# Attention with part of the exponentials on VectorE: four shifted bit patterns summed on TensorE in place of a polynomial, and x transposed by DMA

## The chip, the cores and the metric

One core of one Trainium2 chip. The metric is the time of one execution in microseconds (us), on the device; lower is better. Beside each time stands the mean clock that was granted to TensorE, as a share of full speed: a core at 0.5 all the time multiplies matrices at half speed.

A run is called "slow" here when it is more than 1.5% above the fastest run of the same kernel in its series. On one core that label is no more than this comparison.

The clock is recorded only from its first rise on, which lies between 3.8 and 20.9 us in these traces. Before that the views print full speed, although groups of products follow each other at 0.42 us there, as at half clock. So the mean clocks below are a little too high: with half clock up to the first record, before is 0.614 (not 0.626).

## The reference

```python
B, S, D, H = 1, 2048, 448, 16          # Dh = 28
qkv = (x @ wqkv).reshape(B, S, 3, H, Dh) -> q, k, v      # all bf16
scores = einsum("bhqd,bhkd->bhqk", q, k) * Dh ** -0.5
o = einsum("bhqk,bhkd->bhqd", softmax(scores), v)
return o.reshape(B, S, D) @ wo
```

There are 16 heads of 2048 x 2048 scores, so 67 million exponentials. In tiles of 128 keys by 512 queries that is 1024 tiles. The work is cut into 16 units, each of four heads and 512 queries: 16 key blocks of four tiles, one for each head.

## The kernel before

A small scheduler in the kernel (`P.add`) gives each operation an engine, what it depends on and a priority, and works out the order of each engine. A score tile is one matmul that uses 28 of the 128 rows of the array; three heads run side by side in different row strips. ScalarE takes the exponential of three such tiles in one instruction:

```python
s = P.add("pe", (lambda e, tl=tl, b0=b0: s_mm(e, tl, range(b0, b0 + 3), DH)), ...)
ex = P.add("act", (lambda e, p0=p0, w=w, b0=b0:
           e.activation(PT[:, p0*512:(p0+w)*512], bank(b0, w), AF.Exp, scale=ESCALE)), ...)
```

ScalarE alone would be the bound, so 114 of the 1024 tiles go to VectorE, where a cubic polynomial in the fraction and the integer part make up the bit pattern of a bf16. It takes five instructions for each tile:

```python
o1: DT = min(max(score, ZLO), ZHI)          # PSUM read, to int32
o2: DW = DT.low16 * ES + EC                 # fraction
o3: DU = (DW + EA) * DW
o4: DU = (DU + EB) * DW
o5: PD = DT * (1/512) + DU                  # int16, read as bf16
```

The products with V follow, for a key block at a time: four matmuls side by side, each over 128 rows and in one strip of 32 columns. The same accumulator bank gathers all 16 key blocks of a unit, and a column of ones in V gives the sum of the exponentials.

```python
ins = e.matmul(ps[32*h:32*h+32, ACC*512:(ACC+1)*512], V[:, kt, hh*32:(hh+1)*32],
               p_ap, start=(kt == 0), stop=(kt == NK-1), tile_position=(0, 32*h))
```

x arrives in its natural order and TensorE transposes it through PSUM, the memory that its products are written to: 64 transposes in 16 groups of four.

Of the kernel before, what the change touches and what calls it, by code (L numbers as in the profile page):

```python
# [58 lines left out]
class _Prog:  # L59
# [7 lines left out]
    FULL_CLOCK_UNTIL = 0.0  # L67
# [25 lines left out]
    def pe_dur(self, prev, op, t):  # L93

        if op.kind is None:
            return op.dur
        one, switch = (220.0, 100.0) if t < self.FULL_CLOCK_UNTIL else (430.0, 110.0)
        if prev is None or prev.kind != op.kind:
            return switch + one * op.units
        if op.kind == "r" and op.heads and not set(op.heads) & set(prev.heads):  # L100
            return 60.0
        return one * op.units
# [155 lines left out]
ES = 3.285997142359445e-05  # L258
EC = 27.848949706562973
EA = -77.30729786983042  # L260
EB = 1961.0831047043987
ZLO = -127.0 * 65536.0
ZHI = 128.0 * 65536.0 - 1.0


def _fast(nc, x, wqkv, wo, out, n_heads=16):
# [6 lines left out]
    IT = 112  # L273
    NIT = D // IT
# [7 lines left out]
    NPT = 36  # L282
    NPD = 8
    NDB = 3
# [3 lines left out]
    QSCALE = 65536.0 * LOG2E * scale  # L288
    ESCALE = 1.0 / (65536.0 * LOG2E)
    assert DH * H == D and G * 4 == H and DH + 1 <= 32 and NIT * IT == D and GD <= IT  # L290

# [4 lines left out]
    LATE0, LATE1 = 1, 1  # L296
    ASLACK = 300.0
# [3 lines left out]
    with es:  # L301
# [3 lines left out]
        x_nat = sb("x_nat", [128, NST, D], BF16)  # L305
# [5 lines left out]
        V = sb("V", [128, NK, HC], BF16)  # L311
        PT = sb("PT", [128, NPT * 512], BF16)
        PD = sb("PD", [128, NPD, 512], I16)
        DT = sb("DT", [128, NDB, 512], I32)
        DW = sb("DW", [128, NDB, 512], FP32)
        DU = sb("DU", [128, NDB, 512], FP32)
# [6 lines left out]
        id_b = sb("id_b", [128, 128], BF16)  # L323
# [5 lines left out]
        FLAG = sb("FLAG", [1, 1], I32)  # L329
        ps = es.enter_context(nc.psum_tensor("ps", [128, 8 * 512], FP32))  # L330
# [4 lines left out]
        def bank_bf(b):  # L335
            return ps[:, b * 512:(b + 1) * 512].bitcast(BF16)

        def i32v(ap):
            return ap.bitcast(I32)


        XG = 4
        xv = xf.rearrange("(n p) d -> p n d", p=128)
        wview = wqkv.rearrange("(it p) c -> p it c", p=IT)
        dma_x = []

        def load_x(i, prio):
            n0, n1 = i * NST // XG, (i + 1) * NST // XG
            dma_x.append(P.add("sp", (lambda e: e.dma_start(x_nat[:, n0:n1, :], xv[:, n0:n1, :])),
                               dur=400, prio=prio, name=f"dma_x{i}", dma_group=_DmaGroup(f"x{i}"), nbytes=(n1 - n0) * 128 * D * 2))  # L350
        for i in range(XG):
            load_x(i, -10 + i)
        dma_w = {}
        for t, en, prio in ((1, "act", -20), (0, "act", -19), (2, "sp", -7.5)):
            dma_w[t] = P.add(en, (lambda e, t=t: e.dma_start(w_raw[0:IT, :, t * D:(t + 1) * D], wview[:, :, t * D:(t + 1) * D])),
                             dur=400, prio=prio, name=f"dma_w{t}", dma_group=_DmaGroup(f"w{t}"), nbytes=D * D * 2)


        io_op = P.add("pool", lambda e: e.iota(iota_i[:, :], [[1, 128]], base=0, channel_multiplier=-1),
                      dur=300, prio=-12, name="iota")  # L360
        id_f_op = P.add("dve", lambda e: e.tensor_scalar(id_f[:, :], iota_i[:, :], 0.0, None, ALU.is_equal),
                        deps=[io_op], dur=250, prio=-10, name="id_f")
        id_b_op = P.add("dve", lambda e: e.tensor_copy(id_b[:, :], id_f[:, :]), deps=[id_f_op], dur=150, prio=-10, name="id_b")
        V4 = V.rearrange("p n (hh r) -> p (n hh) r", r=32)
        ms_v0 = P.add("pool", lambda e: e.memset(V4[:, :, DH:32], 0.0), dur=1500, prio=-9, name="ms_v0")
        ms_v1 = P.add("pool", lambda e: e.memset(V4[:, :, VONE:VONE + 1], 1.0), deps=[ms_v0], dur=800, prio=-9, name="ms_v1")
        ms_wop = P.add("pool", lambda e: e.memset(i32v(wop.rearrange("p g d -> p (g d)")), 0), dur=900, prio=-8, name="ms_wop")
        ms_one = P.add("pool", lambda e: e.memset(ONE[:, :], 1.0), dur=100, prio=-7, name="ms_one")
        sel_op = P.add("dve", (lambda e: e.tensor_copy(SEL[:, :], id_f.rearrange("p (h r) -> p h r", r=32)[:, :, VONE])),
                       deps=[id_f_op], dur=100, prio=-6, name="sel")  # L370
        grp_wo = _DmaGroup("wo")
        dma_wo = []
        for g in range(G):
            for h in range(4):
                r0 = (4 * g + h) * DH
                p0 = 32 * h
                dma_wo.append(P.add("sp", (lambda e, g=g, r0=r0, p0=p0: e.dma_start(wop[p0:p0 + DH, g, :], wo[r0:r0 + DH, :])),
                                    deps=[ms_wop], after=dma_wo[-1:] + dma_x[-1:], dur=300, prio=-5, name=f"dma_wo{g}{h}", dma_group=grp_wo))


        P.pool("E", [4, 5, 6])
        P.pool("J", [5, 6])
        P.pool("M", [6])
        early_ev = []
        mid_ev = []
        cur_pool = ["J"]

        def job(name, prio, mm_ops, evac, early, evac_eng="dve", evac_dur=610, after=(), mul=None):

            hold = []  # L390
            prev = None
            pool = "E" if early else cur_pool[0]
            for k, (f, deps, kind, units_) in enumerate(mm_ops):
                op = P.add("pe", (lambda e, f=f: f(e, hold[0].banks[0])),
                           deps=list(deps) + (list(mid_ev if pool == "M" else early_ev) if (k == 0 and not early) else []), after=[prev] + list(after),
                           kind=kind, units=units_, prio=prio if (k == 0 or early) else -4.0, name=f"{name}_{k}", acq=((pool, 1) if k == 0 else None), acq_slack=0.0 if early else ASLACK)
                if k == 0:
                    hold.append(op)
                prev = op
# [6 lines left out]
            ev = P.add(evac_eng, fe, deps=[prev] + list(evac[2:]), dur=evac_dur, prio=prio if early else -100.0, name=f"{name}_ev", rel=[(hold[0], 0)])  # L406
            if pool != "M":
                (early_ev if early else mid_ev).append(ev)
            return ev

        xt_ev = {}

        def tr_job(n0, it, prio, eng):
            def f(e, b):
                ins = None
                for j in range(4):
                    ins = e.transpose(bank_bf(b)[0:IT, j * 128:(j + 1) * 128],  # L417
                                      x_nat[:, n0 + j, it * IT:(it + 1) * IT], id_b[:, :])
                return ins
            xt_ev[(it, n0 // 4)] = job(f"xT{it}_{n0}", prio, [(f, [id_b_op, dma_x[n0 // 4]], "f", 1.1)],  # L420
                                       ((lambda: xT[0:IT, it, n0 * 128:(n0 + 4) * 128]), (lambda b: bank_bf(b)[0:IT, 0:512])),
                                       True, evac_eng=eng, evac_dur=600 if eng == "act" else 420)
# [3 lines left out]
        def proj_qk(t, g, c, prio, early, eng="dve"):  # L426
            dst = KT if t == 1 else QT
            mms = []
            for it in range(NIT):
                def f(e, b, it=it):  # L430
                    ins = None
                    for h in range(4):
                        col = t * D + g * GD + h * DH
                        ins = e.matmul(ps[32 * h:32 * h + 32, b * 512:(b + 1) * 512], w_raw[0:IT, it, col:col + 32],  # L434
                                       xT[0:IT, it, c * 512:(c + 1) * 512], start=(it == 0), stop=(it == NIT - 1), tile_position=(0, 32 * h))
                    return ins
                mms.append((f, [xt_ev[(it, c)]] + ([dma_w[t]] if it == 0 else []), "c", 1.0))
            kq_ev[(t, g, c)] = job(f"p{t}_{g}_{c}", prio, mms,
                                   ((lambda: dst[:, g, c * 512:(c + 1) * 512]), (lambda b: bank(b))), early, evac_eng=eng, mul=QSCALE if t == 0 else None)

        v_ev = {}

        def proj_v(g, c, prio, early):
            mms = []
            for j in range(4):
                n = 4 * c + j

                def f(e, b, j=j, n=n):
                    ins = None
                    for it in range(NIT):  # L450
                        ins = e.matmul(ps[:, b * 512 + j * GD:b * 512 + (j + 1) * GD], xT[0:IT, it, n * 128:(n + 1) * 128],  # L451
                                       w_raw[0:IT, it, 2 * D + g * GD:2 * D + (g + 1) * GD], start=(it == 0), stop=(it == NIT - 1))
                    return ins
                mms.append((f, [xt_ev[(it, c)] for it in range(NIT)] + [dma_w[2]], "f", 1.1))
            Vd = V[:, 4 * c:4 * c + 4, g * 128:(g + 1) * 128].rearrange("p n (h r) -> p n h r", r=32)[:, :, :, 0:DH]
            v_ev[(g, c)] = job(f"pv_{g}_{c}", prio, mms,
                               ((lambda: Vd), (lambda b: bank(b)[:, 0:4 * GD].rearrange("p (n h d) -> p n h d", n=4, d=DH)), ms_v1), early, evac_dur=600)


        for c in range(NCH):  # L460
            for it in range(NIT):
                tr_job(4 * c, it, -3 + 0.25 * c + 0.001 * it if c == 0 else 0.25 * c - 0.35 + 0.001 * it, "act" if (c == 0 and it % 2) else "dve")
            if c == 0:
                proj_qk(0, 0, 0, -2.9, True, "act")
                proj_qk(1, 0, 0, -2.8, True, "dve")
            else:
                proj_qk(1, 0, c, 0.25 * c - 0.3, True)
            proj_v(0, c, 0.25 * c - 0.1, True)
        proj_qk(0, 0, 1, 0.7, True)

        def late_jobs():
            order = [("q", 0, c) for c in range(2, NCH)]
            for g in range(1, G):
                for c in range(NCH):
# [1012 lines left out]
```

## Time and profile before

| | kernel before |
|---|---|
| time, the three first runs | 459.88, 475.35, 478.32 us |
| profiled run | 478.32 us, span 477.6 us, clock 0.626 |
| TensorE busy | 418.7 us, 2985 matmuls |
| ScalarE busy | 419.8 us, 315 exponentials |
| VectorE busy | 387.9 us, 700 instructions |
| first exponential starts, last one ends | 13.1, 456.3 us |

The times fall into two groups, near 460 and near 478, and the profile was taken of a run of the upper group. Three engines are busy above 80%, which tells nothing about which one to relieve.

### The profile page before, as it was taken

The numbers are of one execution on the slowest core, as the hardware profiler recorded it, in microseconds if no ns is written. First come the engines' busy times: TensorE is split into PE (matmuls) and PEld (weight loads), VectorE is DVE, ScalarE is ACT, GpSimd is POOL, SyncE is SP. The second block draws the span as 40 slices with busy tenths as digits, with TensorE's granted clock in tenths as the row PEclk, the third lists the DMA queues.
The fourth block names the chain that finished last, engine by engine and source line by source line (L and its number), as shares of the span: only waits on it lengthen the run. The fifth ranks groups of instructions, "written<-read, shape, count | busy, mean of one in ns | idle before, by whom it ended". The sixth has DMA issues, their size and how long they took to land.

```text
span 477.6 us, 7257 instructions
## 1 busy us (share of the span) xinstructions
PE 418.7 (88%) x2985; PEld 113.1 (24%) x2985; DVE 387.9 (81%) x700; ACT 419.8 (88%) x321; POOL 3.4 (1%) x9
## 2 busy tenths in 40 slices
PE   4999999988999899887999897899888899989775
PEld 2433112121221212121222211121213211122231
DVE  2322499998969899998989899999988899998331
ACT  2766699999999999999999999999999999999810
POOL 2000000000000000000000000000000000000000
PEclk9655555566565657777555758555667756575985
DMA  8100010000000000000001000000001000101111
GB/s 249 32 1 0 1 32 3 1 24 2 23 1 23 3 3 23 3 23 2 25 1 26 1 3 23 15 10 7 19 1 25 0 14 11 26 10 44 49 40 43
DMA packets 13838, 10.09 MB, mean 21 GB/s; under 512 B 5932, under 2 KB 11820, under 8 KB 13800
## 3 DMA queue, kind: packets, MB, share of 16 engines
q1 hardware_dynamic: 12872, 8.78, 6.6%
q10 hardware_dynamic: 928, 0.80, 0.6%
q8 instruction: 24, 0.39, 0.3%
q14 instruction: 14, 0.11, 0.1%
HBM read 7.50 MB, written 2.08 MB: 20 GB/s over the span
## 4 chain that ended last, share of the span: by engine, by line
ACT 41%; PE 40%; DVE 12%; DMA 4%; issue 2%; SPq 0%; ACTq 0%
ACT PT L711 41%; PE ps L698 16%; PE ps L657 8%; PE ps L434 8%; PE ps L451 4%; PE ps L571 3%; DVE DT L731 3%; DVE DU L737 2%; DVE PD L739 2%; DMA w_raw<-in_wqkv_dram 2%; DMA RB<-scr_r 1%; DVE DU L735 1%; PE ps L417 1%; DVE DW L733 1%; DVE OTS L594 1%
## 5 line engine op out<-in xcount | busy, mean ns | idle before, releaser
L711 ACT ACTIVATE PT<-ps 128x1536 bf16<-128x1536 f32 (+1 forms) x315 | 415.6, 1447 | 28.9 <-PE ps L698 26.1
L698 PE MATMUL ps<-QT,KT 28*128 28x512 bf16 x1024 | 208.3, 549 | 42.3 <-ACT PT L711 35.5
L657 PE MATMUL ps<-PT,V 128*32 128x512 bf16 x910 | 132.8, 554 | 0.0
L731 DVE TENSOR_SCALAR DT<-ps 128x512 int32<-128x512 f32 x114 | 78.2, 686 | 15.2 <-PE ps L698 14.7
L698 PEld LDWEIGHTS ps<-QT,KT 28*128 28x128 bf16 x1024 | 40.2, 97 | 209.8 <-ACT PT L711 129.8
L735 DVE SCALAR_TENSOR_TENSOR DU<-DW 128x512 f32<-128x512 f32 x114 | 77.7, 685 | 0.6
L739 DVE SCALAR_TENSOR_TENSOR PD<-DT,DU 128x512 int16<-128x512 int32 x114 | 77.5, 682 | 0.2
L737 DVE SCALAR_TENSOR_TENSOR DU<-DU,DW 128x512 f32<-128x512 f32 x114 | 77.4, 682 | 0.2
L657 PE MATMUL ps<-PD,V 128*32 128x512 bf16 x114 | 61.6, 543 | 0.0
L434 PE MATMUL ps<-xT,w_raw 112*32 112x512 bf16 x512 | 54.7, 556 | 1.9 <-DVE DT L731 0.8
L733 DVE TENSOR_SCALAR DW<-DT 128x512 f32<-128x512 uint16 x114 | 47.3, 420 | 0.6
L657 PEld LDWEIGHTS ps<-PT,V 128*32 128x32 bf16 x910 | 23.9, 102 | 79.0 <-issue 76.1
L451 PE MATMUL ps<-w_raw,xT 112*128 112x112 bf16 x256 | 25.3, 281 | 0.3 <-DVE DT L731 0.3
L405 DVE CAST KT<-ps 128x512 bf16<-128x512 f32 x16 | 11.0, 689 | 15.4 <-PE ps L434 15.2
L583 DVE CAST OUTS<-ps 128x448 bf16<-128x448 f32 x14 | 8.7, 622 | 17.7 <-PE ps L571 17.7
L571 PE MATMUL ps<-wop,OTN 128*128 128x448 bf16 x64 | 20.1, 451 | 3.2 <-DVE OUTS L583 1.2
L451 PEld LDWEIGHTS ps<-w_raw,xT 112*128 112x128 bf16 x256 | 20.8, 134 | 8.5 <-issue 3.9
L405 DVE CAST V<-ps 128x448 bf16<-128x448 f32 x16 | 9.9, 620 | 14.3 <-PE ps L451 14.3
L434 PEld LDWEIGHTS ps<-xT,w_raw 112*32 112x32 bf16 x512 | 14.6, 120 | 27.0 <-issue 16.4
L581 ACT ACTIVATE OUTS<-ps 128x448 bf16<-128x448 f32 x2 | 1.1, 544 | 17.4 <-PE ps L571 17.4
L403 DVE TENSOR_SCALAR QT<-ps 128x512 bf16<-128x512 f32 x15 | 10.3, 687 | 5.4 <-PE ps L434 5.2
L657 PEld LDWEIGHTS ps<-PD,V 128*32 128x32 bf16 x114 | 11.4, 101 | 8.9 <-issue 8.9
(34 smaller groups left out, 68.4 us busy)
## 6 DMA issues: line engine op xcount, KB each, us to landing
RB<-scr_r SPq DMA_DIRECT2D x60, 64.0 KB, 2.0
x_nat<-in_x_dram SPq DMA_DIRECT2D x4, 448.0 KB, 7.9
out_dram<-OUTS SPq DMA_DIRECT2D x16, 112.0 KB, 1.7
w_raw<-in_wqkv_dram ACTq DMA_DIRECT2D x2, 392.0 KB, 6.7
w_raw<-in_wqkv_dram SPq DMA_DIRECT2D x1, 392.0 KB, 9.5
wop<-in_wo_dram SPq DMA_DIRECT2D x16, 24.5 KB
scr_l<-OTS SPq DMA_DIRECT2D x15, 8.0 KB
LT<-scr_l SPq DMA_DIRECT2D x15, 8.0 KB, 1.6
```

The source lines that it names most:

```text
L405: fe = (lambda e: e.tensor_copy(evac[0](), evac[1](hold[0].banks[0])))
L434: ins = e.matmul(ps[32 * h:32 * h + 32, b * 512:(b + 1) * 512], w_raw[0:IT, it, col:col + 32], xT[0:IT, it, c * 512:(c + 1) * 512], start= ...
L451: ins = e.matmul(ps[:, b * 512 + j * GD:b * 512 + (j + 1) * GD], xT[0:IT, it, n * 128:(n + 1) * 128], w_raw[0:IT, it, 2 * D + g * GD:2 * D ...
L571: return e.matmul(bank(hold[0].banks[0])[:, 0:D], OTN[:, gg, n * 128:(n + 1) * 128], wop[:, gg, :], start=(gg == 0), stop=(gg == G - 1))
L657: ins = e.matmul(ps[32 * h:32 * h + 32, ACC * 512:(ACC + 1) * 512], V[:, kt, hh * 32:(hh + 1) * 32], p_ap, start=(kt == 0), stop=(kt == NK ...
L698: ins = e.matmul(bank(b), KT[32 * h:32 * h + rows, g, kt * 128:(kt + 1) * 128], QT[32 * h:32 * h + rows, g, c * QCH:(c + 1) * QCH], start= ...
L711: ex = P.add("act", (lambda e, p0=p0, w=w, b0=b0: e.activation(PT[:, p0 * 512:(p0 + w) * 512], bank(b0, w), AF.Exp, scale=ESCALE)), deps=[ ...
L731: o1 = P.add("dve", (lambda e, T=T, s=s: e.tensor_scalar(T, bank(s.banks[0]), ZLO, ZHI, ALU.max, ALU.min)), deps=[s, d_last[di]], dur=610, ...
L733: o2 = P.add("dve", (lambda e, F16=F16, W=W: e.tensor_scalar(W, F16, ES, EC, ALU.mult, ALU.add)), deps=[o1, d_last[di]], dur=360, prio=pr, ...
L735: o3 = P.add("dve", (lambda e, W=W, U=U: e.scalar_tensor_tensor(U, W, EA, W, ALU.add, ALU.mult)), deps=[o2], dur=610, prio=pr, name=f"D3_{ ...
L737: o4 = P.add("dve", (lambda e, W=W, U=U: e.scalar_tensor_tensor(U, U, EB, W, ALU.add, ALU.mult)), deps=[o3], dur=610, prio=pr, name=f"D4_{ ...
L739: o5 = P.add("dve", (lambda e, U=U, T=T, pi=pi: e.scalar_tensor_tensor(PD[:, pi, :], T, 1.0 / 512.0, U, ALU.mult, ALU.add)), deps=[o4, slo ...
```

## The change

The intent is to take far more of the exponentials away from ScalarE (252 tiles in place of 114) by making one cheaper for VectorE. Read as a bf16, an int16 that grows linearly with the score is a piecewise-linear approximation of an exponential, with an error that repeats with every power of two. Four such patterns, each shifted by a quarter of a power of two (32, 64 and 96 in int16 steps) and weighted, average the error away. The weights go into four scaled copies of V, and TensorE adds the four up in the accumulator. VectorE is left with one read of PSUM for each tile and three cheap 16-bit additions for each four tiles; TensorE gets four V products where it had one.

```diff
+TERM_D = (0, 32, 64, 96)
+TERM_C = (0.25, 0.2099609375, 0.1767578125, 0.1484375)
+ZBIAS = 127.0 * 128.0 - 7.235034912313908
...
-o1 ... o5 (five instructions for each tile)
+r = P.add("dve", e.tensor_scalar(PD[:, zs, 0, h*512:(h+1)*512], bank(...), ZBIAS, 0.0, ALU.add, ALU.max))
+# once the four tiles of the key block are there, for j in 1, 2, 3:
+sh = P.add("dve", e.tensor_scalar(PD[:, zs, j, :], PD[:, zs, 0, :], float(TERM_D[j]), None, ALU.add))
+# and for j in 0 ... 3, head by head:
+pv_mm(e, u, h, VC[:, kt // 4, j, hh*32:(hh+1)*32], PD[:, zs, j, h*512:(h+1)*512].bitcast(BF16))
...
+# which key blocks VectorE takes
+if u == 0: return (3, 7, 15)
+return (3, 7, 11, 15)
...
-tr_job(...)  # TensorE transposes of x and their evictions
+e.dma_start_transpose(xT[:, 0:NIT-1, r0:r1], xf[r0:r1, 0:(NIT-1)*KT_])   # four pairs
...
+for i in range(9):      # all-zero products that start TensorE's clock
+    e.matmul(ps[32*h:32*h+32, ACC*512:(ACC+1)*512], ZW[:, :], ZM[:, :], ...)
...
-P.pool("E", [4, 5, 6]) ; P.pool("J", [5, 6]) ; P.pool("M", [6])
+P.pool("M", [5, 6])     # banks shared by projections, VectorE score tiles, output products
```

ScalarE's groups are now of three and two tiles by turns. Scaling V for the four copies, and the normalising multiply, go to GpSimd.

## The prediction

> **What bounds the kernel now.** I read the page first (busy shares, the slices, the chain), then the groups by shape, then the chain of waits at both ends, then the engines' work in stretches of time.
>
> ```profile
> PE 418.7 (88%) x2985; PEld 113.1 (24%) x2985; DVE 387.9 (81%) x700; ACT 419.8 (88%) x321; POOL 3.4 (1%) x9
> ...
> ACT  2766699999999999999999999999999999999810
> ...
> PEclk9655555566565657777555758555667756575985
> ...
> ACT 41%; PE 40%; DVE 12%; DMA 4%; issue 2%; SPq 0%; ACTq 0%
> ```
>
> Three engines are above 80% busy and the chain is shared by ScalarE (41%) and TensorE (40%). The slices tell them apart by time. From 60 to 444 us ScalarE is at 9 in every slice: there it is the bound. In the first five slices it stands at 6 to 7, and in the last two it is idle. The clock row swings between 5 and 9.
>
> ```profile
> L711 ACT ACTIVATE PT<-ps 128x1536 bf16<-128x1536 f32 x282 | 383.0, 1500 | 14.7 <-PE ps L698 12.4 <-PE ps L657 1.7
> L698 PE MATMUL ps<-QT,KT 28*128 28x512 bf16 x1024 | 208.3, 549 | 42.3 <-ACT PT L711 35.5 <-DVE KT L405 2.3 <-DVE DT L731 1.8
> L657 PE MATMUL ps<-PT,V 128*32 128x512 bf16 x910 | 132.8, 554 | 0.0
> L731 DVE TENSOR_SCALAR DT<-ps 128x512 int32<-128x512 f32 x114 | 78.2, 686 | 15.2 <-PE ps L698 14.7
> ```
>
> Of 1024 score tiles (128x512), ScalarE exponentiates 910, mostly three to an instruction; VectorE does 114 by five instructions each (78.2 + 47.3 + 77.7 + 77.4 + 77.5 = 358 us, 3.14 us a tile). In the timeline 8 ScalarE instructions of three tiles take 10.98 us, so one costs 1.372 us. Check: 282 x 1.372 + 31 x 1.02 (two tiles) + 1 = 420, the busy time.
>
> ```profile
> 24.00:36.00 12.00, 12.00 (x82) 4.79 (x80) 3.21 (x6) 8.18 (x9) 0.00 (x0) 0.50 0.00 1
> ...
> 206.12:209.53 3.41, 3.41 (x33) 1.78 (x30) 3.41 (x7) 3.41 (x3) 0.00 (x0) 0.50 0.24 79
> 209.53:212.95 3.42, 2.47 (x32) 0.73 (x29) 3.42 (x7) 3.20 (x4) 0.00 (x0) 1.00 0.00 0
> ```
>
> The columns are the stretch, its length, then busy us (and instructions) of TensorE, its weight loads, VectorE, ScalarE and GpSimd, then granted clock and DMA. Between 24 and 36 us TensorE is busy all the time at half clock and ScalarE only 8.18 of 12: TensorE bounds the first 60 us. Later the clock jumps between 0.50 and 1.00 on a grid of 3.413 us.
>
> ```profile
> 448.51 5.49 ACT PT L711 x4
> ...
> 462.20 1.98 PE ps L626 x32
> ...
> 474.18 0.54 ACT OUTS L581
> ```
>
> The last exponential ends at 454.0 and the span at 477.6: a tail of 23.6 us.
>
> **What the Trainium skill says.** (1) "TensorE: Matmul & The Clock Gate", Part 1: the clock is half or full, set by activity in windows of about 3.4 us. The trace agrees on both, but plain busy time is not the activity: 12.00 of 12.00 busy stayed at 0.50. I therefore counted, in each of 135 windows, how much array work was streamed, in units of one full 128x128 array over 512 columns (a 28-row score matmul is 0.22, a 32-column V matmul 0.25, and so on). With a limit of 5.8 units the count says what clock the next window gets in 131 of the 135; the mean is 5.04, so this kernel lies just under the limit. (2) "ScalarE: Activation LUTs", What ACT_TABLE_LOAD costs: 186 ns + 0.833 ns an element, with 93 ns of overlap; for 1536 that is 1.373 us, as measured, and for 1024 it gives 0.946. (3) "VectorE: DVE Perf Modes", the perf-mode tier table: a one-source 16-bit SBUF operation over 2048 elements runs four at a time, 693 ns; the trace has none of that kind. (4) "DMA: Bandwidth & Descriptors", table row on DMA transposes: 261 GB/s effective; no run here shows one yet.
>
> **The change part by part.**
>
> *Exponentials.* Unit 0 gives VectorE 3 of its 16 key blocks, the other 15 units give 4: 63 blocks x 4 heads = 252 tiles (114 before). ScalarE keeps 772, in groups of 3 and 2 by turns: 154 x 1.372 + 155 x 0.946 = 358 us, 62 less than 420. This is the gain.
>
> *VectorE.* A block is four PSUM reads (0.60 us apart back to back in the chain) and three shifted copies of 2048 int16. 252 x 0.60 = 151; 189 x 0.60 (estimate: the skill's 693 ns less the 0.09 by which the 686 ns operations overlap) = 114; K and Q evictions 31 x 0.60 = 19, V with its extra copy 12, accumulators 10, outputs 8, reciprocals 4. Sum 318 us against 388: 89% of ScalarE's time. The normalising multiply and the V scaling go to idle GpSimd.
>
> *TensorE.* V groups (four matmuls side by side) rise from 256 to 193 + 4 x 63 = 445. A group streams in 0.427 us at half clock and 0.213 at full (6 groups of the last V products: 1.44 us at full clock, with the fill). At full clock: scores 309 x 0.213 = 66 (the compiled order puts most VectorE score tiles beside a ScalarE group of other heads, nearly free), V 95, K and Q 128 x 0.213 = 27, V projection 14, output 12, end 3: 217; plus some 600 changes of matmul kind at 0.1 us = 60. That is 277 us, hidden under 358. At half clock it is 434 + 60 = 494, which would be the bound.
>
> *The clock.* Array work: scores 224, V 445, K and Q 128, V projection 56, output 56: about 910 units over some 117 windows = 7.8 a window, above 5.8. Where the projections are over (units 11 on, before output products) it is only (2.88 + 1.45) units per 2.318 us of ScalarE = 6.4. So I expect full clock most of the time (0.9 or more) with dips late.
>
> *The start.* Sixteen transposes on TensorE and their evictions go; four pairs of DMA transposes come. Nine dummy products warm the clock. The compiled order has K of block 1 ahead of the first scores, so two x chunks must have landed. I keep the first exponential at 13 us, as before (13.1), but after it the early slices should run at ScalarE's speed, not TensorE's.
>
> *The tail.* The same serial steps, with two PSUM banks for output products where one was (the products 1.67 and evictions 0.64 now overlap) and less half clock: 15 us instead of 23.6.
>
> *Sum.* 13 + 358 + 15 = 386. ScalarE was 96% busy between 60 and 444 us; the new kernel has TensorE at 77%, VectorE at 89% and the two shared banks between them, so I take 96% again: 358 / 0.96 = 373. Total **402 us**.
>
> **Rivals.** *TensorE stays at half clock*: the second-largest sum, 494, becomes the bound and the time is about 500, slower than now. For it: the present kernel holds 0.50 over long stretches with TensorE fully busy. Against: at half clock the V share makes a busy window carry about 0.73 x 8 = 5.9 units, enough to raise it again, and a raised one carries more. A mixture (clock 0.75) gives 415 to 430. *VectorE becomes the bound*: if the int16 copies run one element at a time (2.2 us, from the skill's 1x figure of 2293 ns), VectorE needs 318 + 189 x 1.6 = 620 us. For it: no int16 fast copy in the trace. Against: the condition in the table is 16-bit width. A milder form, GpSimd and VectorE disturbing each other, costs some us. *The DMA transposes are slow*: every us by which chunk 1 lands after about 9 us goes straight into the time; at a third of the rate quoted, 10 us more. *ScalarE loses nothing and was only waiting*: excluded by its 9s.
>
> **Range and chances.** 96% could be 98 (395) or 92 (420); the clock and the start add up to 10 on the bad side. 80%: 388 to 426. The slow rivals together get 4%.
>
> **What would show it.** Right: about 309 exponentials with 358 us busy in all; ScalarE at 9 from the second or third slice on; the clock row mostly 9; V products at about 1780 matmuls with a mean well under 554 ns; the 2048-wide copies near 690 ns; the tail near 15 us. Wrong: a clock row of 5s with TensorE ahead of ScalarE in the chain, or VectorE at 95% and the exponentials waiting for score tiles that wait for a bank, or a first exponential after 18 us.

## The result, and the profile after

| | before | after |
|---|---|---|
| time, four runs each on one chip | 459.88, 475.35, 478.32, 460.60 us | 401.62, 402.29, 400.07, 402.77 us |
| median | 467.98 us | 401.96 us |
| ratio of the fast runs | | 0.874 (0.869 to 0.879) |
| span of the profiled run, clock | 477.6 us, 0.626 | 398.0 us, 0.927 |

A ratio here is the mean time of one kernel's fast runs over that of the other's fast runs of the same rounds. It is therefore not quite the ratio of the medians: the median of before mixes its two groups, the fast runs are those near 460 alone.

The page of the kernel after: busy time, the slices of ScalarE and of the clock, and the shares of the chain of waits.

```profile
PE 348.9 (88%) x3713; PEld 106.6 (27%) x3713; DVE 334.0 (84%) x557; ACT 357.0 (90%) x314; POOL 48.5 (12%) x97
...
ACT  1599999999999999999999999999899999999811
PEclk9899999999999999999968687898689999999886
...
PE 43%; DVE 28%; ACT 24%; DMA 2%; issue 1%; SPq 0%
```

ScalarE stands at 8 or 9 from the third slice until the end of its work; before, the second to fifth slices read 6 and 7 (the first reads 2; the prediction counts it among them). The clock row is made of 9s where it was made of 5s to 7s, with a softer stretch from the 21st to the 30th slice. The chain now goes mostly through TensorE and VectorE although ScalarE is as good as never idle. It is one chain, followed back from the end; where three engines feed one another it can run through any of them, and it does not name the bound here. The slices do.

The groups by shape (busy us, then mean ns of one, then idle time before them and what ended it):

```profile
L741 ACT ACTIVATE PT<-ps 128x1536 bf16<-128x1536 f32 x154 | 231.7, 1505 | 11.4 <-PE ps L704 10.5
L759 DVE TENSOR_SCALAR PD<-ps 128x512 int16<-128x512 f32 x252 | 169.5, 685 | 31.3 <-PE ps L704 29.9
L741 ACT ACTIVATE PT<-ps 128x1024 bf16<-128x1024 f32 x155 | 167.5, 1081 | 0.7 <-PE ps L704 0.4
...
L766 DVE TENSOR_SCALAR PD<-PD 128x2048 int16<-128x2048 int16 x189 | 131.2, 713 | 0.9
L656 PE MATMUL ps<-PD,VC 128*32 128x512 bf16 x1008 | 98.6, 416 | 11.9 <-DVE PD L766 7.9 <-DVE OTS L593 2.4 <-DVE PD L759 0.5
L656 PE MATMUL ps<-PT,V 128*32 128x512 bf16 x772 | 76.5, 408 | 1.1 <-DVE OTS L593 1.1
```

The counts are those that the prediction worked out (154 + 155 exponentials, 252 reads, 189 copies, 1008 + 772 V products). The same V matmul that took 554 ns on average now takes 408: that is the clock, since its shape is unchanged. ScalarE's idle time before its exponentials is 12.1 us in all, where it was 28.9.

The stretch from 24 to 36 us, in the order of columns that the prediction explains:

```profile
24.00:36.00 12.00, 12.00 (x156) 4.42 (x153) 10.12 (x18) 12.00 (x12) 2.60 (x8) 1.00 0.01 3
```

TensorE is busy for the whole stretch, as before, but it does 156 matmuls where it did 82, at a clock of 1.00; ScalarE is busy for 12.00 of 12 us where it was 8.18. Busy time of TensorE said "12.00" in both kernels.

The end of the chain (start, duration, what):

```profile
378.13 4.70 PE ps L570 x16
382.83 0.58 PE ps L656 x8
...
386.73 0.70 DVE OTN L630
387.43 0.05 issue
387.48 4.90 PE ps L570 x16
392.38 0.02 issue
392.40 0.54 ACT OUTS L580
```

The last exponential ends at 379.2 us and the span at 398.0. The tail of 18.8 us holds two sets of output products of nearly 5 us; the first set stands ahead of the last V products.

The profiled runs can be added up. For the kernel before, the tail has to be corrected: the prediction took 454.0 us, the end of the last ScalarE piece on the chain, as the last exponential, but one more, off the chain, ended at 456.3.

| us | before | after | difference |
|---|---|---|---|
| until the first exponential | 13.1 | 13.9 | +0.8 |
| exponentials, busy | 415.6 | 353.8 | -61.8 |
| idle between them | 27.6 | 11.5 | -16.1 |
| after the last one | 21.3 | 18.8 | -2.5 |
| span | 477.6 | 398.0 | -79.6 |

The before of this table is a run of the upper group. Against its fast runs the gain is some 58 us (460.2 to 401.7), and where those runs save their 18 us cannot be read, as none of them has a trace.

### The profile page after: what moved, and what is told of

Read it like the earlier page. It is cut to its first block, busy times and chain, and to the rows that moved or that the text cites. A ratio compares the mean times of both kernels' runs of the same rounds, so it can differ in the third digit from the quotient of the medians.

```text
span 398.0 us, 8639 instructions
## 1 busy us (share of the span) xinstructions
PE 348.9 (88%) x3713; PEld 106.6 (27%) x3713; DVE 334.0 (84%) x557; ACT 357.0 (90%) x314; POOL 48.5 (12%) x97
## 4 chain that ended last, share of the span: by engine, by line
PE 43%; DVE 28%; ACT 24%; DMA 2%; issue 1%; SPq 0%
ACT PT L741 24%; PE ps L656 16%; PE ps L704 16%; DVE PD L759 12%; DVE PD L766 11%; PE ps L430 6%; PE ps L570 2%; PE ps L450 2%; DVE OTS L593 2%; DMA xT<-in_x_dram 2%; DVE QT L410 1%; DVE KT L412 1%; DVE V L412 1%; SPq L349 0%; PE ps L625 0%
## 5 line engine op out<-in xcount | busy, mean ns | idle before, releaser
L741 ACT ACTIVATE PT<-ps 128x1536 bf16<-128x1536 f32 (+1 forms) x309 | 353.8, 1292 | 12.1 <-PE ps L704 10.9
L759 DVE TENSOR_SCALAR PD<-ps 128x512 int16<-128x512 f32 x252 | 169.5, 685 | 31.3 <-PE ps L704 29.9
L704 PE MATMUL ps<-QT,KT 28*128 28x512 bf16 x1024 | 148.2, 407 | 22.6 <-ACT PT L741 19.3
L766 DVE TENSOR_SCALAR PD<-PD 128x2048 int16<-128x2048 int16 x189 | 131.2, 713 | 0.9
L656 PE MATMUL ps<-PD,VC 128*32 128x512 bf16 x1008 | 98.6, 416 | 11.9 <-DVE PD L766 7.9
L656 PE MATMUL ps<-PT,V 128*32 128x512 bf16 x772 | 76.5, 408 | 1.1 <-DVE OTS L593 1.1
L638 POOL TENSOR_TENSOR OTN<-RB,OTS 128x512 bf16<-128x512 f32 x15 | 20.3, 1355 | 199.9 <-DMA RB<-scr_r 199.8
L430 PE MATMUL ps<-xT,w_raw 128*32 128x512 bf16 x512 | 40.7, 397 | 4.4 <-DMA xT<-in_x_dram 4.0
L656 PEld LDWEIGHTS ps<-PD,VC 128*32 128x32 bf16 x1008 | 24.7, 96 | 54.2 <-DVE PD L766 26.8
L465 POOL TENSOR_SCALAR VC<-VX 128x112 bf16<-128x112 f32 x64 | 21.9, 342 | 124.8 <-DVE VX L459 121.8
```

The lines of the kernel that those rows point to most:

```text
L430: ins = e.matmul(ps[32 * h:32 * h + 32, b * 512:(b + 1) * 512], w_raw[:, it, col:col + 32], xT[:, it, c * 512:(c + 1) * 512], start=(it == ...
L465: sc = P.add("pool", (lambda e, dst=dst, j=j: e.tensor_scalar(dst, src, TERM_C[j], 1.0, ALU.mult, ALU.mult)), deps=[ev2, ms_c1[j]], after= ...
L638: nm = P.add("pool", (lambda e: e.tensor_tensor(OTN[:, g, c * QCH:(c + 1) * QCH], RB[:, ub, :], OTS[:, ub, :], ALU.mult)), deps=[l4], dur= ...
L656: return e.matmul(ps[32 * h:32 * h + 32, ACC * 512:(ACC + 1) * 512], lhsT, rhs, start=first, stop=False, skip_group_check=True, tile_posit ...
L704: return e.matmul(bank(b), KT[32 * h:32 * h + DH, g, kt * 128:(kt + 1) * 128], QT[32 * h:32 * h + DH, g, c * QCH:(c + 1) * QCH], start=Tru ...
L741: ex = P.add("act", (lambda e, p0=p0, w=w, b0=b0: e.activation(PT[:, p0 * 512:(p0 + w) * 512], bank(b0, w), AF.Exp, scale=ESCALE)), deps=[ ...
```

## The experiments

Twelve kernels ran. The first series shared a chip and the runs of before there (seven runs, 458.1 to 463.1 us).

One count is used throughout. For every window of 3.413 us (the grid on which the clock changes) I added up the array work that was streamed, in array units (one full 128 x 128 array over 512 columns), as the prediction did, now also with the transposes in it (with them, the kernel before has 5.18 a window; the prediction, without them, had 5.04). The rule "5.8 units or more, and the next window gets the full clock" then tells the next clock right in 1673 of 1731 windows of fourteen traces. The limit was set on the trace of before alone. A recount gave 1697 of 1745; there, "the clock stays as it is" is right in 1449, and the best of six limits tried on TensorE's busy time in 1138. Few windows at half clock are left in the fast kernels (16 in after, 11 in c_d3zero, 9 in a_spread), so their shares in the fifth column rest on little.

| kernel | array units in the windows counted | a window | a window at half clock | of those, followed by full clock | clock |
|---|---|---|---|---|---|
| before | 699 | 5.18 | 4.83 | 13% | 0.626 |
| a_rows72 | 706 | 5.08 | 4.46 | 4% | 0.607 |
| b_dmaT | 715 | 5.34 | 4.92 | 17% | 0.657 |
| a_d2 | 803 | 6.13 | 4.62 | 10% | 0.690 |
| a_d5 | 948 | 6.67 | 5.04 | 17% | 0.745 |
| a_d3 | 862 | 6.74 | 5.28 | 30% | 0.757 |
| b_dummy | 943 | 7.14 | 5.47 | 28% | 0.822 |
| after | 907 | 8.02 | 6.05 | 69% | 0.927 |
| c_d3zero | 1019 | 8.49 | 6.23 | 64% | 0.953 |
| a_spread | 891 | 8.33 | 6.16 | 56% | 0.959 |

(The windows before the first record of the clock are left out of the count. The traces hold all of the products: 713 units for before, 920 for after and for a_spread.)

### a_rows72: the same instructions, fewer rows of the array

Every V product reads 72 of its 128 rows. The result is wrong; the instructions, their columns and their order stay the same (the traces show TensorE's products in the very same order). If the clock follows instructions or busy time, nothing happens; if it follows the filled array, it must fall.

```diff
-return e.matmul(ps[...], lhsT, rhs, start=first, ...)
+return e.matmul(ps[...], lhsT[0:72], rhs[0:72], start=first, ...)
```

> The changed kernel with every V product contracted over 72 of the 128 rows (wrong result on purpose): the same instructions, shapes of output and streaming time, but the array work of a V group falls to 0.56 units. Theory (the clock of the next 3.413 us follows the array work, and the changed kernel needs the clock): late stretches carry (1.62 + 1.45) units per 2.318 us = 4.5 a window, below 5.8, so half clock there and partly before; mean clock 0.6 to 0.75; TensorE then needs 2.6 to 3.2 us per five ScalarE tiles against 2.318, time 425 to 455 us. Rival (the clock follows busy time, or ScalarE hides TensorE at any clock): 402 us and an unchanged clock of 0.93.

Measured: 453.58, 471.76, 483.33 and 495.24 us at clocks of 0.699, 0.652, 0.633 and 0.607: the lower the clock, the longer the run. Even the fastest is 52 us above the kernel after. From the page and the windows of the profiled run (495.24 us):

```profile
PEclk9999555598555555555975555555555555556866
...
L656 PE MATMUL ps<-PD,VC 72*32 72x512 bf16 x1008 | 133.6, 574 | 2.6 <-DVE OTS L593 1.5
L656 PE MATMUL ps<-PT,V 72*32 72x512 bf16 x772 | 104.9, 559 | 0.8 <-DVE OTS L593 0.8
```

```profile
24.00:48.00 24.00, 23.75 (x293) 8.54 (x293) 21.41 (x38) 23.89 (x22) 3.74 (x12) 0.99 0.02 4
48.00:72.00 24.00, 24.00 (x177) 5.82 (x170) 15.64 (x27) 16.54 (x14) 2.40 (x5) 0.50 0.08 18
```

Up to 48 us, while many products of the projections run beside it (119 from 24 to 48 us), the clock is full and ScalarE is at 23.89 of 24. In the next stretch, with 45 of them, TensorE is busy for all of 24.00 us at 0.50, and ScalarE falls to 16.54. So it is the rows of the array that count, and nearly the whole gain of the change hangs on the clock: with the offload in place but the clock lost, the kernel is about where it was before, or slower. The direction and the clock came as expected; the time went above the range in three of four runs. The range was too narrow for the clock that went with it: a mean of 0.6 means half clock for 80% of the time.

### b_dummy: the clock without the offload

The opposite arm. In the kernel before, each V product but a unit's last is followed by a group of four products of zeros, which change no result, and its scheduler is told of a full clock throughout and of V groups that take twice as long, so that TensorE's order changes too.

```diff
+if kt < NK - 1:
+    for h in range(4):
+        ins = e.matmul(ps[32*h:32*h+32, ACC*512:(ACC+1)*512], ZW[:, :], ZM[:, :], start=False, stop=False, ...)
...
-P.FULL_CLOCK_UNTIL = 45000.0
+P.FULL_CLOCK_UNTIL = 1e9
```

> The kernel before with a group of four all-zero V products added behind each V group but a unit's last (240 groups, result unchanged) and its static order made for the full clock. Array work rises from 5.0 to about 6.8 units a window. Theory (clock by array work; the kernel before is bound by ScalarE from 60 us on): clock 0.9 or more, the first 60 us shorten by some 15 us, the tail by 4; the middle stays: 445 to 455 us. Rival (the higher clock is what made the changed kernel fast): 400 to 415 us. Third (zeros do not count as work, the added products only cost): clock 0.6 and 480 us or more.

Measured: 456.48 (fast, clock 0.871), 467.99, 470.08 and 472.42 us (slow, 0.805 to 0.822), beside fast runs of before at 456.98 to 462.48, mean 460.0. Fast against fast that is a ratio of 0.992, from a single fast run.

```profile
ACT  2999898998899999899898999988997999999950
...
PEclk9999795955899597598879979555877989798995
```

The clock rose from 0.63 to 0.82, and ScalarE stands at 8 and 9 from the second slice on, so the early loss is mended. Little came of it. ScalarE still needs 414 us for its exponentials, which with a start of 12.4 and a tail of 17.0 makes 444 even without one idle microsecond. I had expected 445 to 455; it missed that, and the remaining half-clock stretches, in which the zeros themselves take TensorE's time, are in the row above. So a higher clock alone brought some 4 us, by one fast run at 0.871; a clock that is full throughout was not reached, and the sum above leaves some 15 us at most for it. Neither half of the change gains much alone, the two together gain 58.

### a_d2, a_d3: fewer key blocks for VectorE

Two and three key blocks for each unit in place of four (one less in unit 0).

```diff
-    return (3, 7, 15)
-return (3, 7, 11, 15)
+    return (7, 15)                # a_d3;  a_d2: (7,)
+return (3, 7, 15)                 # a_d3;  a_d2: (7, 15)
```

> The changed kernel with half the key blocks on VectorE (2 a unit, 1 in unit 0: 124 tiles, about as many as the kernel before gave it); ScalarE keeps 900 tiles, 180 pairs x 2.318 us = 417 us. Theory (the gain is ScalarE's smaller share): the changed kernel needs 402 for 358 us of ScalarE work, so 36 us of ends and 2% of gaps; here 417 x 1.022 + 36 = 462 us, clock 0.6 to 0.8 because the array work falls to some 6.2 units a window. Rival (the gain is the clock, the DMA transposes or the shorter VectorE sequence, whatever the share): 400 to 415 us.

> 3 blocks a unit (2 in unit 0): 188 VectorE tiles, ScalarE 836 = 387.5 us of work. Theory: 387.5 x 1.022 + 36 = 432 us, half way between. Rival: as for a_d2, 400 to 410 us.

Measured: a_d2 468.02 us (467.74 to 470.44, ratio 1.016 [1.012 to 1.021]), a_d3 447.57 us (447.13 to 449.52, ratio 0.972 [0.967 to 0.976]). ScalarE's busy time steps down evenly (417.9, 389.0, 357.0 us for two, three and four blocks), the time does not: 20 us from two to three, 45 from three to four. a_d2 came out 6 us above what I expected and a_d3 15 us. The clock row of a_d3, and two stretches of its windows:

```profile
PEclk8899999999999956666665655666566565869886
```

```profile
192.00:240.00 48.00, 41.25 (x315) 8.18 (x311) 26.71 (x42) 44.87 (x40) 2.87 (x2) 0.64 0.04 13
240.00:300.00 60.00, 53.22 (x373) 10.15 (x373) 33.74 (x53) 54.68 (x47) 3.03 (x2) 0.59 0.04 11
```

Once the projections thin out, the clock falls to 0.6 and ScalarE loses 3 to 5 us in each stretch. For each unit of the kernel's work, a_d3 has 14 array units of scores and 13 + 12 of V products beside 52 ScalarE tiles (some 24.1 us, 7.05 windows): 5.5 a window, just under 5.8, where four blocks have 6.4. That explained the miss, but only by argument; the next experiment tests it.

### c_d3zero: a_d3 with useless work added

From unit 4 on, each ScalarE V product of a_d3 is followed by four products of zeros: 156 groups more for TensorE to do, and no result changed. The scheduler is told that these products take twice as long, which changes TensorE's order from there on.

```diff
-op = P.add("pe", f, ..., units=1.0, ...)
+op = P.add("pe", f, ..., units=2.0 if (u >= 4 and name[:2] == "PV") else 1.0, ...)
...
 ins = pv_mm(e, u, h, V[:, kt, hh*32:(hh+1)*32], PT[:, slots[h]*512:(slots[h]+1)*512])
+if u >= 4:
+    for h in range(4):
+        ins = pv_mm(e, u, h, ZW[:, :], ZM[:, :])
```

> The version with three VectorE blocks a unit ran in 447 us where 432 had been expected: its clock is 1.00 up to 120 us and about 0.6 in the stretches from 192 to 360 us. Worked out per unit it has 14 score units and 13 + 12 V units of array work for 52 ScalarE tiles (24.1 us, 7.05 windows): 5.5 a window, just under the limit of 5.8, where four blocks have 6.4. Here every ScalarE V product from unit 4 on is followed by one group of four products of all-zero operands, which changes no result and lifts that to 7.2. Theory (the clock alone cost the 15 us): the clock goes above 0.9, ScalarE takes 389 us / 0.97 = 401 us, with 15 at the start and 17 at the end 433, and 2 to 3 of start-up: 436 (432 to 440). Rival (VectorE, the banks or the order of the groups cost it, and more TensorE work can only make it worse): 447 or more whatever the clock.

Measured: 422.16 us (420.57 to 425.64, six runs), ratio 0.918 [0.912 to 0.924], clock 0.95 to 0.97; correct.

```profile
PEclk9899999999999999899889699997989999999996
...
L656 PE MATMUL ps<-ZM,ZW 128*32 128x512 bf16 x624 | 63.6, 398 | 0.0
```

```profile
192.00:240.00 48.00, 39.51 (x413) 9.38 (x409) 28.72 (x44) 45.23 (x41) 2.75 (x2) 0.87 0.05 13
240.00:300.00 60.00, 48.65 (x532) 11.53 (x528) 34.74 (x56) 58.06 (x52) 3.82 (x3) 0.93 0.06 15
```

TensorE does 98 and 159 more matmuls in these two stretches and is busy for less time (39.51 and 48.65 us against 41.25 and 53.22). ScalarE's idle time before its exponentials is 8.3 us over the whole kernel, where a_d3 had 30.1. The rival, that more TensorE work can only make it worse, is out: 63.6 us of additional work for an engine that looked 88% busy made the kernel 25 us faster. That the new order has a share in this is not excluded, as the zeros were not tried in the old order. It beat even my own 436. I had put 401 us between the first and the last exponential (all of ScalarE's 389 us of a_d3, at 97%); it is 388.3, as the exponentials take only 380.5 us, and fill 98% of it.

There are now two kernels that hold the clock. From c_d3zero to a_spread (below) ScalarE's busy time falls from 383.7 to 354.7 us and the time from 422.2 to 394.2: 28.0 us for 29.0. Between these two, with the clock held, a microsecond off ScalarE is a microsecond off the kernel.

### a_d5: one block more than the change

Five key blocks for each unit, with up to two VectorE tiles beside one ScalarE group. The sums come out wrong in this version; it is for the time alone.

```diff
-return (3, 7, 11, 15)
+return (3, 7, 11, 14, 15)
...
-nxt = gi + 1
+nxt = gi + (len(slots) % 2)
```

> 5 blocks a unit (312 VectorE tiles; the fifth block uses the scaled V of its neighbour, so the result is wrong on purpose); ScalarE falls to 330 us of work. Theory: VectorE is close behind ScalarE in the changed kernel and becomes the bound: 312 x 0.67 + 234 x 0.69 + 33 = 404 us of work, time about 440 us, ScalarE idle 20% of the span. Rival (ScalarE alone is the bound, VectorE has room): 330 x 1.022 + 36 = 373 us.

Measured: 487.30 us (clock 0.789), 500.72, 503.57 and 507.86 us (0.740 to 0.757). Both expectations missed. One stretch of the profiled run (503.57 us), and its chain:

```profile
48.00:72.00 24.00, 24.00 (x154) 4.64 (x150) 16.31 (x28) 16.00 (x14) 1.26 (x1) 0.50 0.07 18
```

```profile
PE 63%; DVE 30%; ACT 3%; DMA 1%; issue 1%; SPq 0%
```

The kernel gets stuck at half clock with TensorE busy for 24.00 of 24 us, and ScalarE does 16.00. More V work is there than in the kernel after (948 units in the windows counted, against 907), yet a half-clock window carries 5.04 units, and only 17% of them are followed by a full one, against 69% after. My reading is a trap: at half clock what counts is the most that a fully busy TensorE can bring into a window, and a VectorE tile that finds no group of other heads to run beside takes a slot of its own for 0.22 units. The two edits were not tried apart, so why the half-clock window is thinner is argued, not shown. The trace has one more difference: from 48 to 72 us not one product of a projection runs, where the kernel after has 68; whether that is the cause or comes of it stays open. That five blocks are worse than four, by 85 us even in the fastest run, is shown for this schedule only; which part of it does the harm stays open.

### b_dmaT: the DMA transposes alone

The front end of the change (four pairs of DMA transposes, weights in 128-row pieces) put into the kernel before, with nothing else.

```diff
-e.dma_start(x_nat[:, n0:n1, :], xv[:, n0:n1, :])      # and 64 transposes on TensorE
+e.dma_start_transpose(xT[:, 0:NIT-1, r0:r1], xf[r0:r1, 0:(NIT-1)*KT_])
```

> The kernel before with only the front end of the change: x transposed by DMA into 128-row blocks, no transposes on TensorE and no evictions of them. Theory: its first 60 us are bound by TensorE at half clock, which loses 64 transposes (64 x 0.107 + 16 changes of kind x 0.1 = 8.5 us); the first exponential stays at 13 to 14 us: 8 us less, 455 to 462 us where the kernel before has 460 to 478. Rival: the DMA transposes delay the start by as much as they save: no change.

Measured: 475.21 to 477.54 us in four runs, ratio 1.040 [1.032 to 1.047] to the fast runs of before. The eight runs of before beside it were four at 457 to 462 and four at 478 to 481; the four of this kernel lie with the upper group, and what puts a run there I don't know (the mean clock does not: in the last series the upper runs had 0.701 to 0.716, the lower ones 0.666 to 0.705). So a loss of 4% is not established, and against the upper runs alone (mean 479.3) these are 2 us shorter. The gain of 8 us that I expected is not there by either measure, and the trace says why:

```profile
24.00:36.00 12.00, 12.00 (x86) 3.03 (x82) 1.92 (x4) 8.25 (x9) 0.00 (x0) 0.50 0.00 0
```

Removing the transposes leaves TensorE at half clock and busy for the whole early stretch, and ScalarE does 8.25 of 12 us where it did 8.18. The first exponential starts at 14.1 us against 13.1. What made the early slices of the kernel after fast was the clock, not the missing transposes: b_dummy, which keeps them, has fast early slices too.

### a_nowarm, a_tail, a_spread, and the kernel after itself as control

One series of six runs each, on one chip.

```diff
-for i in range(9):       # a_nowarm: the zero products at the start
+for i in range(1):
```

```diff
-out_proj(c*NQT + j, pr + 0.2*j, ...)                               # a_tail: output products of
+out_proj(c*NQT + j, (17.0 if u == NU-2 else pr) + 0.2*j, ...)      # unit 14 after the last V products
```

```diff
-pr = 0.7 + i / 4.0       # a_spread: the 39 late projections, one for every 0.29 units,
+pr = 0.7 + i / 3.4
+while job_first and job_first[0][0] <= pos + LATE_LAG:     # and none earlier than 0.6 units
+    job_first.pop(0)[1].after.append(s)                    # ahead of its place
```

> The changed kernel itself, as the control of the next three: 402 us.

> The changed kernel with one instead of nine dummy groups at the start. Theory: the warmed window (5.5 to 8.9 us) passed before x landed at 9.24 us and the first projection ran at half clock anyway: 402 us, no change. Rival (they shorten the start): 404 to 406 us.

> The changed kernel with the output products of the last unit but one placed behind the last V products and not ahead of them. Theory: 4.7 us of products between the last exponential (379.2) and the last V product (382.8) held the end up by 3 us: 399 us. Rival: they only move behind and cost the same there: 402 us.

> The changed kernel with its 39 projection jobs spread over the units (none ahead of its place in the ScalarE stream), so that the array work no longer runs out at 192 us. Theory: ScalarE lost 5.4 us between 192 and 300 us because the clock dipped to 0.67 to 0.86 there; with work spread, windows stay above 5.8 units, clock 0.97 or more: 397 to 400 us. Rival (these gaps come from waits for PSUM banks and VectorE, not from the clock): 402 us with a flat clock.

| | median, us | range | ratio to before | clock of the profiled run |
|---|---|---|---|---|
| a_ctrl | 402.63 | 395.82 to 408.81 | 0.867 [0.860, 0.873] | 0.922 |
| a_nowarm | 401.23 | 400.06 to 405.38 | 0.873 [0.868, 0.878] | 0.927 |
| a_tail | 400.40 | 394.00 to 403.95 | 0.862 [0.854, 0.870] | 0.913 |
| a_spread | 394.23 | 392.34 to 398.46 | 0.856 [0.851, 0.862] | 0.959 |

The zero products at the start are worth nothing that these runs can see, as expected. Their trace shows why: they end at 5.2 us, and the full clock that follows is recorded from 5.5 to 9.0 us, but between 5.2 and 8.9 TensorE was busy for 0.01 us, waiting for x. The projections that follow at 9.2 start at half clock again.

a_tail lies within the spread of the control, though its tail is 16.2 us where the control has 17.7. a_spread was expected at 397 to 400 and came out at 394. In the kernel after, the projections run ahead as fast as TensorE has room and are over at 189 us; spread out, they last until 270 us. Two stretches after 192 us, first of the kernel after, then of a_spread:

```profile
192.00:240.00 48.00, 41.16 (x385) 9.51 (x377) 39.86 (x65) 45.48 (x40) 2.68 (x2) 0.79 0.05 13
240.00:300.00 60.00, 47.96 (x455) 11.50 (x452) 48.69 (x79) 57.12 (x51) 2.54 (x2) 0.83 0.04 11
```

```profile
192.00:240.00 48.00, 43.03 (x488) 13.41 (x488) 44.94 (x76) 47.48 (x42) 7.04 (x14) 0.96 0.05 14
240.00:300.00 60.00, 49.44 (x562) 14.27 (x562) 54.01 (x88) 58.73 (x53) 5.44 (x7) 0.97 0.06 16
```

The clock in them goes from 0.79 and 0.83 to 0.96 and 0.97, and ScalarE regains 2.0 and 1.6 us. Over the whole kernel its idle time between the exponentials is 7.2 us, where the kernel after has 11.5. The order of TensorE differs as well, so the share of the clock in this is read from the stretches and not tested apart. The 95% intervals of a_spread and the control overlap by a hair (up to 0.862, from 0.860), so 1.2% by the fast runs is likely rather than certain; the next run came out the same again.

### c_best: both small changes

> Both small changes of the third set of runs together: the projections spread over the units (394.2 alone) and the first fifteen units' output products moved behind the last V products (400.4 alone against 402.6 for the control, inside the noise). If the gains add, 392 (391 to 394), tail about 16 us and clock 0.95 or more. Rival: the tail's order is worth nothing, 394 to 395.

Measured: 395.17 us (392.74 to 395.91, six runs), ratio 0.858 [0.854 to 0.863], correct. It is the same as a_spread, so the order at the end adds nothing that shows. (The edit moves the output products of unit 14 alone, not of fifteen units as the expectation says.) The first output products did go behind part of the last V products, and the tail became 16.7 us (17.5 in a_spread); that is less than the spread of the runs. Either version beats both kernels; a_spread is the simpler one.

## Why the prediction was right

**The total.** It was 402 us (its terms add up to 401, and its bounds for 98% and 92% to 393 and 417, where it says 395 and 420), and the median of four runs is 401.96. The agreement to a tenth is luck: the terms were off and cancelled. Start 13 predicted, 13.9 in the profiled run. Main stretch 358 / 0.96 = 373 predicted, 365.3 measured, as the exponentials need 353.8 us and are 97% of it. Their cost was misread: where they follow one another closely, the starts are 1.330 us apart for three tiles and 0.903 for two (medians of 149 and 121 pairs in the kernel after), and not 1.372 "as measured" and 0.946. The 10.98 us that the prediction divided by eight hold the full length of the last one, its check compared with all of ScalarE's work (419.8) and not with the exponentials (415.6), and the overlap of 93 ns that it took from the Trainium skill ("ScalarE: Activation LUTs", What ACT_TABLE_LOAD costs) is some 43 ns less than these starts show. Tail 15 predicted, 18.8 measured. And 3.6 us lie between the span (398.0) and the time (401.62), which my sum had not asked about; the profiled run of before has only 0.7 there, its later runs 1.8, the other versions 1.7 to 4.7, and I don't know why. In all +0.9 - 7.7 + 3.8 + 3.6 = +0.6 on a sum of 401.

**The gain is the exponentials.** Confirmed as a size: -61.8 us of busy time against the -62 of the prediction (both of its terms were some 4 us too high). The runs add a condition that the prediction states only among its rivals: the gain is there with a high clock and gone or cut without it (a_rows72; a_d3 against c_d3zero), and between the two kernels that hold the clock ScalarE's saving arrives one to one (28.0 us for 29.0).

**The clock.** This was the boldest step, from a limit found in one trace: 7.8 units a window, so "0.9 or more with dips late". Measured 8.02 and 0.927, with the dips between 200 and 300 us, where the projections are over. They were over at 189 us, in unit 7 (counted from 0), and not from unit 11 on as the prediction had it, so the thin stretch was longer. And a mean above the limit is not enough: a_d2, a_d3 and a_d5 have 6.1 to 6.7 a window and stay between 0.69 and 0.76. The escape from half clock was also worked out: a busy half-clock window would carry about 5.9 units. Measured 6.05, and 11 of those 16 windows were followed by a full one. The rival "TensorE stays at half clock" was put near 500 us; a_rows72 and a_d5 show that this state exists (453 to 508 us). It was closer than "the slow rivals together get 4%" suggests: one key block less brings the late stretch under the limit.

**VectorE.** Sum 318 us predicted, 334.0 measured, mostly in the shifted copies: 131.2 us for 189, where I had 114. Their own speed was right, and three back to back take 1.89 us with starts 0.60 apart. But the overlap of 0.09 that I subtracted exists only where something follows at once. And the rival's "milder form, GpSimd and VectorE disturbing each other" is there: the 18 copies that overlap the normalising multiply on GpSimd average 976 ns, one took 1767, against 682 for the 159 that meet no GpSimd work; that is some 5 us. ScalarE's slices stay at 8 and 9, so I count nothing of this in the total, but no run tests it.

**TensorE.** The 277 us, 77% of ScalarE's time, were too low; it is busy for 348.9 us, 98% of ScalarE's 357.0. The 277 us had full clock throughout. It did little harm, as most of it was beside ScalarE's time; a_spread, with a steadier clock after 192 us, is some 8 us faster than its control.

**The start.** Sized right for a partly wrong reason. The transposes by DMA took 3.7 to 7.0 us each to land (265 GB/s moved between 5.2 and 8.9 us, but the weights are among them, so the 261 that the prediction quoted for transposes is neither confirmed nor refuted) and did not bring what was expected of them (b_dmaT), nor did the warming products (a_nowarm).

**The tail.** The mis-sized term. I counted on two banks to take output products at "less half clock"; two sets of sixteen products at 4.70 and 4.90 us stand in the chain, one of them ahead of the last V products. a_tail, which puts that one behind them, has a tail of 16.2 us (the control 17.7, the kernel after 18.8), so its place explains a part of the miss at most; the rest stays open.

## What to carry to other kernels

When TensorE is "busy" at half clock, count the filled array, not busy time: rows times columns streamed in each window of the clock's grid. The count told here which changes would pay, why one block fewer lost most of the gain, and that work for filling (even zeros, better still useful work kept back for the thin stretch) can shorten a kernel whose TensorE already looks busy. And an offload from the bounding engine and the clock of the engine that takes the work should be judged together: here neither gave more than one or two per cent without the other (a_rows72, b_dummy).

## What the Trainium skill lacked or had wrong

- "TensorE: Matmul & The Clock Gate", Part 1, gives full clock after a busy window of some 3.4 us. Busy time is not what counts: 24.00 of 24 us busy stayed at 0.50 (a_rows72, 48 to 72 us), and fewer rows with the same instructions brought the clock from 0.93 to between 0.61 and 0.70. A limit of about 5.8 full-array units in a window of 3.413 us told the next clock right in 1673 of 1731 windows. Products of zeros count in full: in c_d3zero the count is right in 121 of 121 windows with them at full weight, in 103 at half weight, in 92 without them.
- "VectorE: DVE Perf Modes", perf-mode tier table, has times for bf16 and fp32 only; the page's condition is 16-bit width, so what is missing is a measured time for int16. A one-source int16 operation over 2048 elements in SBUF takes 682 ns here when no GpSimd work overlaps it, the same tier as its bf16 entry, and starts can be 0.60 us apart.
- "SBUF — State Buffer", Terms, says that VectorE and GpSimd hold a shared port pair exclusively. The trace agrees in kind and gives a size for one pair of operations, which the page lacks: 976 ns on average and 1767 at most, in place of 682, for the 18 copies that overlapped a GpSimd multiply of 512 columns. Six of the 18, all begun inside a multiply, took 1159 to 1767 and ended about 0.55 us after it; the other twelve took 677 to 770. Reads from PSUM beside the same multiply stayed at 686 ns.
